# First expert's weights and two token tiles prepared in small pieces during the first MoE, no GpSimd sums from the border on, and second products taken as they are ready

## The chip, the core and the metric

One NeuronCore of one Trainium2 chip. The metric is the device time of one launch in microseconds; the kernel before has a median of 2106.39 us over three runs.

## What is computed

Three stages follow one another: causal attention with a decay bias, a dense MLP called here the first MoE, and an eight-expert MoE with balanced gates called the second MoE.

```python
def reference(q, k, v, s, w_in, w_out, w_gate, w1, w2):
    x = attention(q, k, v, s)               # 4 batches, 8 heads, 576 tokens, 64 wide
    x = x.transpose(0, 2, 1, 3).reshape(2304, 512)
    h = x @ w_in                            # 512 -> 2048
    x = (h * sigmoid(1.702 * h)) @ w_out    # 2048 -> 512
    logits = x @ w_gate                     # 8 experts
    P = np.exp(logits - logits.max())
    for _ in range(8):                      # rows and columns in turn
        P /= P.sum(1, keepdims=True) + 1e-9
        P /= P.sum(0, keepdims=True) + 1e-9
        P *= 2304 / 8
    out = 0
    for e in range(8):
        out += P[:, e:e+1] * (np.maximum(x @ w1[e], 0) @ w2[e])   # 512 -> 1024 -> 512
    return out
```

## The kernel before

The kernel is one program with five instruction streams. It does not issue its instructions where they are written: each call goes to a **planner** (class `Sequencer`, lines 51 to 246). The planner keeps a clock per engine and costs per operation (`cost`, line 120), holds DVE, ACT, POOL and SP operations back, and issues them in order of time; PE operations are issued at once. Of several operations that could go, the one of lower `rank` goes first, then the older one. `rank` 2 is for preparation that may wait. From `begin_second` on, `seq.fine` picks finer costs. All instructions therefore have one helper line in the profile, L261, and tiles tell them apart. On the chip each engine runs its own stream in the order the planner left, and semaphores do the waiting.

**Attention and first MoE** (to about 578 us of the span). PE takes attention units, transposes and MoE products as they come ready. The 2304 tokens of the first MoE are nine blocks of 256; the first seven run one by one. For a block and one of eight pairs of 256 hidden units, `mm1` makes `hp` (24 matmuls of 256 columns), ACT makes a tanh into `t`, DVE multiplies it with `hp`, ACT or DVE rounds it into `gh`, POOL subtracts for the rest `gl` (`any_less`), and `mm2` (line 984) adds 24 products into `acc`. The finished block goes through a tile `xo`, in the two-buffer ring `st` of `mpool`, to HBM (`x2_d`). The same ring, once the first MoE's weights are converted (about 190 us), is used to find the scales of expert 0's weights (`first_scales`, `more_scales`): eight loads of 512 KB, each with a DVE maximum.

**The border** (578 to 687 us). The last two blocks run together with 512 columns (`wide1`, `wide2`, lines 1019 to 1056): sixteen half pairs, each 12 matmuls into `hp` and 12 into `accw`. Beside them the planner places, at rank 2, what expert 0 needs: `prep_x(0)` and `prep_x(1)`, `prep_w2(0)`, `prep_w1(0, 0)`, `prep_w1(0, 1)` and then `weight_scales(1)`. A preparation loads four quarter matrices, forms the sums of a seven-product scheme (`seven`, `prep_w1`, `prep_x`), and turns each of the seven operands into a high and a low 16-bit half: ACT scales and rounds, DVE or POOL subtracts. For expert 0 the sums go to DVE or POOL, whichever has the shorter queue (`of_two`).

**Second MoE** (687 us on). For each of 8 experts and 3 token tiles of 768 there are four `unit1` (x times w1, seven products of 6 matmuls with 384 columns) and three `unit2` (h times w2, seven products of 12 matmuls with 256 columns). Two units are active at a time, on two sets of four PSUM banks A to D, and PE alternates between them by readiness. The seven results are combined by copying a bank and adding on to it: bank B starts as a copy of A, and C as a copy of B. Inside `unit2` (line 1504) the order of the products is written out: M1 (A), M7 (D), M2 (A), M6 (B), M5 (C), M4 (D), M3 (C). Only M1 and M7 may stop before the last quarter of `h`. The next expert's weights are prepared at rank 2 from `after1`: `weight_scales(e+1)` after tile 0, `prep_w2(e+1)` after tile 1, and `prep_w1(e+1, half)` after tile 2. Expert 0's start is different: `prep_x(2)` has rank 3 and comes first.

Of the kernel before, what the change touches and what calls it, by code (L numbers as in the profile page):

```python
# [9 lines left out]
F32 = mybir.dt.float32  # L10
# [21 lines left out]

POOL_BIAS = 3000
# [17 lines left out]
class Sequencer:  # L51
# [51 lines left out]
    def where(ap):  # L103
# [5 lines left out]
        hi = lo + sum((n - 1) * abs(st) for st, n in pairs[1:]) + 1  # L109
        return (p0, p0 + pairs[0][1]), (lo, hi)  # L110
# [9 lines left out]
    def cost(self, engine, what, out, ins):  # L120
        n = max(self.size(x) for x in [out] + ins[:2])
        psum = any(x.space == PSUM for x in ins)
        if self.fine:
            if engine == "PE":
                return self.size(out) * (4 if ins[0].dtype == F32 else 1) / 2.4 + (13 if ins[0].dtype == F32R else 5)
# [20 lines left out]
    def submit(self, engine, what, call, outs, ins):  # L146
# [8 lines left out]
        else:  # L155
            op.cost = self.cost(engine, what, outs[0], ins)
# [146 lines left out]
def kernel(  # L303
# [35 lines left out]
    early = const.tile([128, 41], F32, name="early")  # L339
# [10 lines left out]
    border = ExitStack()  # L350
# [633 lines left out]
    def mm2(i):  # L984
# [18 lines left out]
        if p == last and i == 1:  # L1003
# [3 lines left out]
            for m in range(2):  # L1007
                xo = mpool.tile([128, 2, TB1], F32, tag="st", name="xo", bufs=2)
# [27 lines left out]
    def wide2():  # L1036
# [8 lines left out]
        for m in range(KC):  # L1045
# [3 lines left out]
            if last:  # L1049
                xo = mpool.tile([128, 2, TB1], F32, tag="st", name="xo", bufs=2)  # L1050
# [155 lines left out]
    def first_scale(key, cols):  # L1206
# [9 lines left out]
        nc.vector.tensor_scalar(out=w[:, 1:2], in0=w[:, 0:1], scalar1=FLOOR, scalar2=None, op0=ALU.max)  # L1216
        b = w.bitcast(I32)
        nc.vector.tensor_scalar(
# [10 lines left out]

    def first_scales():  # L1230

        for i in range(8):
            st = mpool.tile([128, 1024], F32, tag="st", name="wm", bufs=2)
            if i < 4:
                v, s_ = "p (c f) -> p c f", w1[0, :, i * 256:(i + 1) * 256].rearrange("(c p) f -> p c f", p=128)
                st_ = st.rearrange(v, c=4)
            else:
                r = (i - 4) * 256
                st_ = st.rearrange("p (c d) -> p c d", c=2)
                s_ = w2[0, r:r + 256, :].rearrange("(c p) d -> p c d", p=128)  # L1240
            nc.sync.dma_start(out=st_, in_=s_)
            nc.vector.tensor_reduce(
                out=early[:, i:i + 1], in_=st, axis=AX.X, op=ALU.max, apply_absolute_value=True
            )
            yield st
            if i % 4 == 3:
                yield first_scale(("w1" if i < 4 else "w2", 0), early[:, i - 3:i + 1])
        q_of[0] = early[:, 40:41]
# [804 lines left out]
```

## Time and profile before

| | |
|---|---|
| runs | 2106.39, 2097.49, 2107.42 us (median 2106.39) |
| profiled execution | 2094.25 us, span 2092.5 us |
| PE busy | 1970.6 us (94%), 15782 matmuls recorded |
| DVE, ACT, POOL busy | 1407.9 us (67%), 1250.8 us (60%), 457.5 us (22%) |
| DMA | 317 MB, 152 GB/s on average |
| chain that ended last | PE 50%, issue 24%, DVE 11%, DMA 7%, POOL 4%, ACT 3% |

PE is the busiest engine; its matmuls are pipelined and their ends modelled, so a busy PE may still run below its best pace. A per-stage reading needs the stretches: before 190 us, to 578, to 687, to 950 and the rest. The engine names are PE (TensorE), DVE (VectorE), ACT (ScalarE), POOL (GpSimd) and SP (the queue that issues DMAs).

### The profile page before, as it was taken

The numbers are of one execution on the slowest core, as the hardware profiler recorded it, in microseconds if no ns is written. First come the engines' busy times: TensorE is split into PE (matmuls) and PEld (weight loads), VectorE is DVE, ScalarE is ACT, GpSimd is POOL, SyncE is SP. The second block draws the span as 40 slices with busy tenths as digits, with TensorE's granted clock in tenths as the row PEclk, the third lists the DMA queues.
The fourth block names the chain that finished last, engine by engine and source line by source line (L and its number), as shares of the span: only waits on it lengthen the run. The fifth ranks groups of instructions, "written<-read, shape, count | busy, mean of one in ns | idle before, by whom it ended". The sixth has DMA issues, their size and how long they took to land.

```text
span 2092.5 us, 41023 instructions
## 1 busy us (share of the span) xinstructions
PE 1970.6 (94%) x15782; PEld 1565.2 (75%) x15782; DVE 1407.9 (67%) x2927; ACT 1250.8 (60%) x2540; POOL 457.5 (22%) x473
## 2 busy tenths in 40 slices
PE   4888999999998999989999999999999999999998
PEld 3787999999986667756777777777767677777776
DVE  8987664754367656867875775675786677577555
ACT  5876554654445656565765656666676665566544
POOL 7775343453266121000001000000000000000000
PEclk9999999999999999999999999999999999999999
DMA  7554422331067635555666667648657566765331
GB/s 223 165 165 146 124 64 73 112 93 57 17 173 247 155 136 177 193 181 153 202 212 123 192 204 157 172 125 219 167 146 219 125 165 178 149 194 155 128 124 51
DMA packets 206232, 317.11 MB, mean 152 GB/s; under 512 B 20436, under 2 KB 134932, under 8 KB 206036
## 3 DMA queue, kind: packets, MB, share of 16 engines
q1 hardware_dynamic: 193076, 290.89, 43.8%
q0 software_dynamic: 12960, 23.60, 8.9%
q8 instruction: 124, 2.03, 0.4%
q14 instruction: 72, 0.59, 0.1%
HBM read 229.20 MB, written 80.68 MB: 148 GB/s over the span
## 4 chain that ended last, share of the span: by engine, by line
PE 50%; issue 24%; DVE 11%; DMA 7%; POOL 4%; ACT 3%; SPq 1%; POOLq 0%; ACTq 0%; DVEq 0%
PE C L261 9%; PE D L261 8%; PE A L261 7%; PE hp L261 7%; PE acc L261 6%; PE B L261 4%; DVE h L261 2%; PE sp L261 2%; POOL acc_d L261 2%; PE tp L261 2%; PE op L261 2%; DVE t L261 2%; DMA w_d<-wo 1%; DMA wm<-in_moe_w_dram 1%; DMA xc_d<-xo 1%
## 5 line engine op out<-in xcount | busy, mean ns | idle before, releaser
L261 PEld LDWEIGHTS <-h 128*128 128x128 f16 x6048 | 591.2, 98 | 134.7 <-issue 33.3
L261 PEld LDWEIGHTS <-w1o 128*128 128x128 f16 x4036 | 395.5, 98 | 270.8 <-issue 12.1
L261 POOL DMA_DIRECT2D acc_d<-y x90 | 77.9, 884 | 1050.9 <-DVE y L261 961.8
L261 PE MATMUL D<-xt,w1o 128*128 128x384 f16 x1152 | 218.9, 328 | 10.2 <-ACT w1o L261 8.2
L261 PE MATMUL A<-w2o,h 128*128 128x256 f16 x1728 | 216.2, 272 | 10.4 <-ACT B L261 10.4
L261 PE MATMUL C<-w2o,h 128*128 128x256 f16 x1728 | 210.1, 274 | 15.5 <-ACT C L261 12.2
L261 PE MATMUL D<-w2o,h 128*128 128x256 f16 x1728 | 220.7, 273 | 0.5 <-DVE h L261 0.5
L261 PE MATMUL C<-xt,w1o 128*128 128x384 f16 x1152 | 218.5, 326 | 1.9 <-DVE hst L261 1.2
L261 PE MATMUL A<-xt,w1o 128*128 128x384 f16 x1152 | 216.0, 326 | 0.3 <-DVE sc L261 0.3
L261 DVE SCALAR_TENSOR_TENSOR h<-hst,h 128x768 f16<-128x768 f32 (+1 forms) x192 | 144.3, 760 | 45.0 <-ACT h L261 42.9
L261 PE MATMUL hp<-xh,wih 128*128 128x256 f32 (+1 forms) x512 | 155.5, 304 | 3.9 <-DVE t L261 3.9
L261 PE MATMUL hp<-xl,wih 128*128 128x256 f32 (+1 forms) x512 | 153.0, 299 | 0.0
L261 PE MATMUL hp<-xh,wil 128*128 128x256 f32 (+1 forms) x512 | 152.8, 298 | 0.0
L261 ACT ACTIVATE h<-hst 128x768 f16<-128x768 f32 (+1 forms) x192 | 128.8, 678 | 6.7 <-DVE hst L261 6.7
L261 POOL TENSOR_TENSOR gl<-t,gh 128x512 fp32r<-128x512 f32 x72 | 96.9, 1346 | 159.8 <-ACT gh L261 109.5
L261 PE MATMUL B<-w2o,h 128*128 128x256 f16 x864 | 107.8, 275 | 15.6 <-DVE h L261 9.6
L261 ACT ACTIVATE sm<-sm,stats 64x576 f32<-64x576 f32 (+4 forms) x160 | 93.3, 602 | 43.9 <-DVE stats L261 42.9
L261 ACT ACTIVATE hst<-A 128x384 f32<-128x384 f32 x96 | 47.0, 489 | 121.2 <-PE A L261 120.4
L261 PE MATMUL acc<-gh,woh 128*128 128x256 f32 x384 | 111.0, 289 | 0.0
L261 PE MATMUL B<-xt,w1o 128*128 128x384 f16 x576 | 110.3, 328 | 0.0
L261 ACT ACTIVATE t<-hp 128x512 f32<-128x512 f32 x72 | 42.8, 594 | 112.5 <-PE hp L261 111.3
L261 ACT COPY B<-A 128x384 f32<-128x384 f32 (+1 forms) x168 | 70.5, 422 | 64.7 <-PE A L261 64.3
(243 smaller groups left out, 4254.4 us busy)
## 6 DMA issues: line engine op xcount, KB each, us to landing
xt<-xc_d SPq DMA_DIRECT2D x168, 384.0 KB
wr<-in_moe_w_dram SPq DMA_DIRECT2D x128, 256.0 KB
w_d<-wo SPq DMA_DIRECT2D x112, 256.0 KB
wm<-in_moe_w_dram SPq DMA_DIRECT2D x112, 256.0 KB
w2o<-w_d SPq DMA_DIRECT2D x56, 512.0 KB
acc_d<-y POOLq DMA_DIRECT2D x90, 256.0 KB, 5.6
kq<-in_qk_dram SPq DMA_DIRECT2D x32, 448.0 KB
kq<-in_qk_dram SPq DMA_DIRECT2D x32, 256.0 KB
```

Source lines behind the costliest of these rows:

```text
L261: self.seq.submit(self.name, what, lambda: method(*args, **named), outs, ins)
```

## The change

1. **Early pieces.** `first_scales` now also prepares expert 0 in the first MoE: w2 in four pieces and w1 in four (operands of 256 columns), then token tiles 0 and 1 in four pieces each (192 columns). A piece takes both buffers of the ring `st`; one loads, the other holds seven results that go to HBM. In pieces all sums and low halves are on DVE. The eight maxima for the scales become ACT squares.
2. **Border.** `prep_x(0)`, `prep_x(1)`, `prep_w2(0)` and `prep_w1(0, ..)` are gone from it; w1 of expert 0 is loaded ready from HBM in 14 transfers. `xo` moves from ring `st` to ring `t`.
3. **No POOL sums** from the border on: with `seq.fine`, `any_less` (and with it `gl`) is on DVE, and so are all sums.
4. **Expert 1 sooner.** `prep_w2(1)` is queued before expert 0 begins, with `prep_x(2)` ahead of it at rank 1.
5. **Products as ready.** `unit2` asks after each product which of those left is ready, in the order M1, M7, M2, M4, M6, M5, M3; every product may stop before the last quarter of `h`.
6. **Planner.** A range is counted in bytes, an operation with two outputs costs 190 more, and a fine PE matmul 2.7 instead of 5 above its columns. Sums reuse their inputs' buffers.

```diff
     def any_less(out, a, b, bias=POOL_BIAS):
-        engine = nc.vector if seq.load("DVE") + bias <= seq.load("POOL") else nc.gpsimd
+        engine = nc.vector if seq.fine or seq.load("DVE") + bias <= seq.load("POOL") else nc.gpsimd
...
     def of_two(out, in0, in1, op):
-        engine = nc.vector if seq.load("DVE") <= seq.load("POOL") else nc.gpsimd
-        engine.tensor_tensor(out=out, in0=in0, in1=in1, op=op)
+        nc.vector.tensor_tensor(out=out, in0=in0, in1=in1, op=op)
...
-                xo = mpool.tile([128, 2, TB1], F32, tag="st", name="xo", bufs=2)
+                xo = mpool.tile([128, 2, TB1], F32, tag="t", name="xo", bufs=2)
...
     def first_scales():
+        yield from early_scales(0)
+        for j in range(NJ):
+            yield early_w2(0, j)
+        for half in range(2):
+            for c in range(2):
+                yield early_w1(half, c)
+        yield from early_x(0)
+        yield from early_x(1)
...
+    def early_w2(e, j):
+        a, b = staged("wa"), staged("wb")
+        for fh in range(2):
+            r = fh * (F2 // 2) + j * 128
+            nc.sync.dma_start(out=a[:, fh * 512:fh * 512 + 512], in_=w2[e, r:r + 128, :])
...
+        def part(i, src):
+            o = out_slot(b, 256, 256, count_[0]).rearrange("p (h d) -> p h d", h=2)
+            count_[0] += 1
+            in_two(o[:, 0], o[:, 1], src, sc)
+            nc.sync.dma_start(out=w2_d[e % 2][i][:, :, j], in_=o)
+        seven([a[:, q * 256:q * 256 + 256] for q in range(4)], part, b[:, 0:256])
+        return b
...
     def begin_second():
-        prep_x(0)
...
-        prep_w2(0)
-        mem["raw"], mem["wo"] = (mem["ep"], 7), (mem["ep"], 2)
-        prep_x(1)
...
     def begin_weights():
         load_x2(0)
-        prep_w1(0, 0)
-        prep_w1(0, 1)
-        seq.rank = 3
-        weight_scales(1)
+        for half in range(2):
+            w1s[0, half] = pool.tile([128, 7, 2, 2, 256], F16, tag="w1o", name="w1o", bufs=2)
+            for i in (0, 6, 5, 3, 4, 1, 2):
+                nc.sync.dma_start(out=w1s[0, half][:, i], in_=w1_d[half][i])
+        second_expert()
...
     load_w2(0)
-    seq.rank = 3
+    seq.rank = 1
     prep_x(NTP - 1)
+    seq.rank = 2
+    prep_w2(1)
...
-        if tp == 1 and e + 1 < E:
+        if tp == 1 and 0 < e < E - 1:
             later(2, prep_w2, e + 1)
...
+        while todo:
+            yield lambda: min(x[0] for x in choices())
+            every = list(choices())
+            soon = max(min(x[0] for x in every), seq.free["PE"])
+            t, name, part = next(x for x in every if x[0] <= soon)
...
+            prod(bank[role], k, n, first=not before_, part=part)
+            if part[-1] == NJ - 1:
+                todo.remove(name)
+                after(name, bank[role])
+            else:
+                half_done.add(name)
```

How the streams move at three places follows; a row is one instruction with its tiles and size, in the order of its engine.

DVE at the border, early in the wide stage. `t` and `hp` belong to the first MoE, `wo`, `wr` and `wt` to expert 0's w2, `xo`, `xr` and `xt` to token tile 0. Before:

```order
L261 SCALAR_TENSOR_TENSOR t<-t,hp 128x512
L261 CAST gh<-t 128x512
L261 SCALAR_TENSOR_TENSOR wo<-wr,early,wo 128x512
L261 SCALAR_TENSOR_TENSOR wo<-wt_8791,early,wo 128x512
L261 TENSOR_TENSOR xo_8762<-xr,xo_8762 128x384
L261 SCALAR_TENSOR_TENSOR t<-t,hp 128x512
L261 CAST gh<-t 128x512
L261 TENSOR_TENSOR xo_8769<-xr,xo_8769 128x384
L261 SCALAR_TENSOR_TENSOR wo<-wr,early,wo 128x512 x2
L261 TENSOR_TENSOR xt_8768<-xt_8767,xr 128x384
L261 TENSOR_TENSOR xr<-xr 128x384
```

The same place now, where `xa` and `xb` are the two buffers of a piece of token tile 1:

```order
L263 SCALAR_TENSOR_TENSOR t<-t,hp 128x512
L263 TENSOR_TENSOR gl<-t,gh 128x512
L263 TENSOR_TENSOR xb<-xa,xb 128x192 x2
L263 SCALAR_TENSOR_TENSOR t<-t,hp 128x512
L263 TENSOR_TENSOR gl<-t,gh 128x512
L263 SCALAR_TENSOR_TENSOR t<-t,hp 128x512
L263 TENSOR_TENSOR xa<-xa 128x192 x2
L263 TENSOR_TENSOR gl<-t,gh 128x512
L263 TENSOR_TENSOR xb<-xa,xb 128x192 x2
L263 TENSOR_TENSOR xa<-xa 128x192
L263 TENSOR_TENSOR xb<-xa,xb 128x192 x3
L263 TENSOR_TENSOR xa<-xa 128x192
```

The rows of expert 0's weights are gone, `gl` has come over from POOL, and two of tile 1's four pieces are still here; later in the stage only `t`, `gh` and `gl` are left.

DVE at the start of expert 1. `hst`, `h`, `sa` and `sb` belong to a `unit1`; `w1o`, `wr` and `ws` are expert 1's second half of w1, which PE's third `unit1` of the expert reads. Before:

```order
L261 SCALAR_TENSOR_TENSOR w1o_11641<-wr_11645,sc5_9294,w1o_11641 128x512
L261 TENSOR_TENSOR h_12213<-sb_12215,h_12213 128x768
L261 TENSOR_TENSOR ws_11647<-wr_11642,ws_11646 128x512
L261 TENSOR_TENSOR wr_11644<-wr_11642,wr_11644 128x512
L261 TENSOR_TENSOR wr_11643<-wr_11643,ws_11647 128x512
L261 SCALAR_TENSOR_TENSOR w1o_11641<-ws_11646,sc5_9294,w1o_11641 128x512
L261 SCALAR_TENSOR_TENSOR w1o_11641<-ws_11647,sc5_9294,w1o_11641 128x512
L261 SCALAR_TENSOR_TENSOR w1o_11641<-wr_11644,sc5_9294,w1o_11641 128x512
L261 SCALAR_TENSOR_TENSOR w1o_11641<-wr_11643,sc5_9294,w1o_11641 128x512
L261 SCALAR_TENSOR_TENSOR hst_12283<-D0_12260,u2_12267 128x384
```

Now, at the first two `unit1` of expert 1 (`hst` of D0, then of D1):

```order
L263 SCALAR_TENSOR_TENSOR hst_12296<-D0_12265,u2_12272 128x384
L263 SCALAR_TENSOR_TENSOR w1o_11859<-wr_11862,sc5_9582,w1o_11859 128x512
L263 SCALAR_TENSOR_TENSOR hst_12296<-C0_12284,m7_12273 128x384
L263 SCALAR_TENSOR_TENSOR w1o_11859<-wr_11860,sc5_9582,w1o_11859 128x512
L263 SCALAR_TENSOR_TENSOR w1o_11859<-wr_11863,sc5_9582,w1o_11859 128x512
L263 SCALAR_TENSOR_TENSOR w1o_11859<-ws_11864,sc5_9582,w1o_11859 128x512
L263 TENSOR_TENSOR wr_11861<-wr_11861,wr_11860 128x512
L263 SCALAR_TENSOR_TENSOR h_12354<-hst_12296,h_12354 128x384
L263 TENSOR_TENSOR sa_12355<-hst_12296 128x384
L263 SCALAR_TENSOR_TENSOR h_12354<-hst_12296,h_12354 128x768
L263 SCALAR_TENSOR_TENSOR hst_12375<-D1_12333,u2_12340 128x384
```

Before, the third unit's join (`hst_12283`, the fifteenth join in all) stood behind five `w1o` rows; now one `w1o` row is left behind the fourteenth join.

PE inside the first pair of `unit2` of a later expert's tile, around the first matmul of M6 (bank B of set 1). The number behind `h` is one of the four quarters of the hidden width; 21214 before and 21388 now are the last. Before:

```order
L261 LDWEIGHTS h_21214
L261 MATMUL D0_21288<-w2o_20268,h_21214 128x256
L261 LDWEIGHTS h_21214
L261 MATMUL D0_21288<-w2o_20268,h_21214 128x256
L261 LDWEIGHTS h_20981
L261 MATMUL B1_21284<-w2o_20268,h_20981 128x256
```

Now:

```order
L263 LDWEIGHTS h_21388
L263 MATMUL D1_21425<-w2o_20443,h_21388 128x256
L263 LDWEIGHTS h_21388
L263 MATMUL D1_21425<-w2o_20443,h_21388 128x256
L263 LDWEIGHTS h_21153
L263 MATMUL B1_21469<-w2o_20443,h_21153 128x256
```

Before, M6 came right behind the last quarter of M7 (D0); now the 12 matmuls of M2 (bank A of set 0) and the 12 of M4 (D1) stand between that quarter and M6.

## Rows read from the trace of the kernel before

**Rows 1.** Busy time of each engine by stretch (x: instructions), granted clock, DMA share.

```profile
100.00:190.00 90.00, 76.93 (x733) 69.85 (x731) 80.34 (x195) 68.23 (x139) 61.35 (x58) 0.98 0.52 159
190.00:578.00 388.00, 386.01 (x3778) 368.63 (x3779) 212.43 (x674) 195.07 (x368) 155.98 (x177) 0.99 0.27 80
578.00:687.00 109.00, 97.13 (x417) 76.99 (x416) 75.40 (x93) 56.60 (x116) 65.86 (x47) 0.97 0.67 209
687.00:850.00 163.00, 153.41 (x1247) 109.57 (x1247) 108.81 (x221) 95.13 (x197) 21.66 (x19) 0.98 0.49 151
850.00:950.00 100.00, 83.19 (x623) 61.80 (x621) 68.83 (x147) 58.63 (x126) 0.00 (x0) 0.93 0.60 198
950.00:1950.00 1000.00, 970.34 (x7344) 716.76 (x7343) 694.33 (x1241) 639.53 (x1325) 77.91 (x90) 1.00 0.64 170
```

**Rows 2.** Timeline of PE in the border (start, us), then the gate's matmuls.

```profile
581.68 0.40 PE L261 MATMUL hp<-xh,wih 128*128 128x512 f32 x1
...
611.17 0.39 PE L261 MATMUL accw<-gh,woh 128*128 128x512 f32 x1
...
613.89 0.39 PE L261 MATMUL hp<-xh,wih 128*128 128x512 f32 x1
...
L261 PE MATMUL gp<-wgs,xt x180: 169/169/221, 687.0 to 821.7; 128*128 128x16 f16 x180
```

**Rows 3.** What PE waited for, 578 to 687 us (total us, times, longest).

```profile
PE accw L261 <- POOL gl L261: 8.5, 8, 2.1
PE accw L261 <- DVE gh L261: 3.3, 2, 1.8
```

**Rows 4.** What PE waited for, 687 to 950 us.

```profile
PE D L261 <- ACT w1o L261: 8.2, 1, 8.2
PE A L261 <- ACT B L261: 4.2, 4, 3.1
PE B L261 <- ACT h L261: 4.1, 3, 1.8
...
PE B L261 <- DVE h L261: 2.5, 3, 1.3
...
PE D L261 <- DVE w1o L261: 1.0, 1, 1.0
```

**Rows 5.** Busy time by stretch of 10 us, where PE stood longest.

```profile
900.00:910.00 10.00, 4.53 (x14) 1.92 (x15) 6.89 (x11) 4.19 (x7) 0.00 (x0) 0.50 0.49 151
```

**Rows 6.** What PE waited for, 950 us to the end.

```profile
PE C L261 <- ACT C L261: 11.4, 12, 2.3
PE B L261 <- DVE h L261: 7.1, 11, 0.8
...
PE B L261 <- ACT h L261: 1.9, 5, 0.4
```

**Rows 7.** Groups of instructions, shapes apart: busy us, mean ns of one, idle before.

```profile
L261 DVE SCALAR_TENSOR_TENSOR w1o<-wr,sc,w1o 128x512 f16<-128x512 f32 x70 | 50.2, 745 | 1.1 <-ACT w1o L261 1.1
L261 DVE SCALAR_TENSOR_TENSOR y<-C,pq,y 128x256 f32<-128x256 f32 x63 | 30.4, 482 | 113.8 <-PE C L261 92.6 <-ACT m L261 12.4 <-ACT y L261 7.5
L261 DVE SCALAR_TENSOR_TENSOR w1o<-wr,early,w1o 128x512 f16<-128x512 f32 x10 | 13.4, 1368 | 4.3 <-ACT w1o L261 4.3
L261 DVE TENSOR_REDUCE early<-wm 128x1 f32<-128x1024 f32 x8 | 9.7, 1218 | 4.8 <-DMA wm<-in_moe_w_dram 4.8
L261 DVE TENSOR_TENSOR ws<-wr 128x512 f32<-128x512 f32 x14 | 9.6, 684 | 0.5 <-DMA wr<-in_moe_w_dram 0.5
L261 ACT ACTIVATE wm<-wm 128x512 f32<-128x512 f32 x112 | 69.2, 621 | 32.2 <-DMA wm<-in_moe_w_dram 32.1
L261 ACT ACTIVATE y<-C,pq 128x256 f32<-128x256 f32 x62 | 29.0, 468 | 117.8 <-PE C L261 110.8 <-DVE y L261 6.9
```

**Rows 8.** POOL's costliest group, in the same view.

```profile
L261 POOL TENSOR_TENSOR gl<-t,gh 128x512 fp32r<-128x512 f32 x72 | 96.9, 1346 | 159.8 <-ACT gh L261 109.5 <-DVE gh L261 39.1 <-issue 4.1
```

**Rows 9.** DMA issues on SP: duration of one issue, ns min/median/max, first and last start.

```profile
L261 SPq DMA_DIRECT2D xc_d<-xo x42: 319/322/571, 593.1 to 802.3; - x42
```

More of the change, by code (lines that the diff above doesn't have):

```diff
@@ new lines, in one_scale, with early_x, out_slot @@
+    def one_scale(key, cols, squares=False):
+        if "small" in mem:
+            scale_of(key, cols, squares)
+        else:
+            yield first_scale(key, cols, squares)
+    def early_x(tp):
+        yield 3 * tp + 3
+        yield from one_scale(("x", tp), xmx[:, 6 * tp:6 * tp + 6])
+        for c in range(2):
+            for q in range(2):
+                yield early_x_part(tp, c, q)
+    def out_slot(b, at, n, i):
+        return b[:, at + i % (5 if n == 192 else 3) * n:][:, 0:n].bitcast(F16)
@@ new lines, in early_w1, with part @@
+    def early_w1(half, c):
+        a, b = staged("wa"), staged("wb")
+        piece = {}
+        for fh in range(2):
+            for kh in range(2):
+                x = a[:, (2 * fh + kh) * 256:(2 * fh + kh) * 256 + 256]
+                r, f0 = (2 * kh + c) * 128, fh * (F2 // 2) + half * 256
+                nc.sync.dma_start(out=x, in_=w1[0, r:r + 128, f0:f0 + 256])
+                piece[fh, kh] = x
+        sc = sc_of["w1", 0]
+        count_ = [0]
+        def part(i, src):
+            o = out_slot(b, 256, 256, count_[0]).rearrange("p (h d) -> p h d", h=2)
+            count_[0] += 1
+            in_two(o[:, 0], o[:, 1], src, sc)
+            nc.sync.dma_start(out=w1_d[half][i][:, :, c], in_=o)
+        four(piece, part, b[:, 0:256])
+        return b
@@ L1568, in unit2 @@
         before = {}
-        most, last = range(NJ - 1), range(NJ - 1, NJ)
-        yield ready(0, 0, free("A"), part=most)
-        past[s] = False
-        a = bank_tile("A", s)[:, 0:256]
-        prod(a, 0, 0, part=most)
-        yield ready(3, 6, free("D"), part=most)
-        d = bank_tile("D", s)[:, 0:256]
-        prod(d, 3, 6, part=most)
-        yield ready(0, 0, part=last)
-        prod(a, 0, 0, part=last)
-        b = bank_tile("B", s)[:, 0:256]
-        nc.scalar.copy(out=b, in_=a)
@@ L1581, in unit2 @@
-        y0, y1 = (mem["st"].tile([128, DM], F32, tag="y", name="y", bufs=4) for _ in range(2))
-        whole_d = ready(3, 6, part=last)
-        done_d = whole_d() <= seq.free["PE"]
-        if done_d:
-            prod(d, 3, 6, part=last)
-            put(y1[:, 256:512], d, t1)
-        yield ready(2, 1, settled(a))
-        prod(a, 2, 1, first=False)
-        put(y0[:, 0:256], a, t0)
-        past[s] = True
-        if not done_d:
-            yield whole_d
-            prod(d, 3, 6, part=last)
-            put(y1[:, 256:512], d, t1)
@@ L1608, in unit2, with of, add @@
-        leave(t1, y1)
-        yield ready(6, 2, settled(c))
-        prod(c, 6, 2, first=False)
-        put(y0[:, 256:512], c, t0)
-        leave(t0, y0)
+        bank, y, begun = {}, {}, set()
+        def of(t, half):
+            if t not in y:
+                y[t] = mem["st"].tile([128, DM], F32, tag="y", name="y", bufs=4)
+            return y[t][:, half * 256:half * 256 + 256]
+        def add(o, t, half):
+            if (t, half) in begun:
+                more(of(t, half), o, t)
+            else:
+                begun.add((t, half))
+                put(of(t, half), o, t)
@@ new lines, in unit2, with at @@
+        steps = {
+            "M1": ("A", 0, 0, ()), "M7": ("D", 3, 6, ()), "M2": ("A", 2, 1, ("M1",)), "M4": ("D", 1, 3, ("M7",)),
+            "M6": ("B", 5, 5, ("M1",)), "M5": ("C", 4, 4, ("M6",)), "M3": ("C", 6, 2, ("M5",)),
+        }
+        todo = list(steps)
+        half_done = set()
+        def at(name, part):
+            role, k, n, before_ = steps[name]
+            if any(x in todo for x in before_):
+                return never
+            if name in half_done or before_:
+                t = ok(bank[role])
+            else:
+                t = bank_free(role, s)
+            return max(t, ready(k, n, part))
```

241 lines of the change are left out of this document (143 added, 98 removed).

## The prediction

> **What bounds the kernel now.** I read the busy time by stretch first, then what PE waited for in each, then the groups with shapes apart for prices. The stretches say where PE has something to lose [rows 1]. From 190 to 578 us, attention and first MoE, it is busy 386.0 of 388.0 us: it sets the pace, and DVE (212.4 us, 55%) and ACT (195.1 us, 50%) hide beside it. The border, 578 to 687 us, leaves it idle 11.9 of 109 us; 687 to 950 us, expert 0 and the start of expert 1, 9.6 and 16.8 us; the thousand behind that 29.7 us, 3%. So the time lies in the border and expert 0, and there is little anywhere else.
>
> Border: the first wide matmul starts at 581.68 us, the gate's first at 687.0 us, 105.3 us later. At full pace 12 of them take 613.89 - 611.17 = 2.72 us [rows 2], so the 16 x 24 take 87.0 us. 18.3 us are lost: 11.8 in waits, of them 8.5 for `gl` on POOL [rows 3], the rest in a granted clock of 0.97 and in starts. Expert 0 to 950 us: 9.2 us for expert 1's `w1o`, 4.2 for the copy of A into B, 6.6 for parts of `h` [rows 4]; in the 10 us of the long wait the granted clock is 0.50, that is the lower of the two levels, 1.2 GHz [rows 5], after an idle stretch; PE is busy 4.53 us there, so about 2.3 us of it are the clock's. Later: 9.0 us of waits of bank B for `h`, 11.4 us for the copy of B into C [rows 6].
>
> **The change, part by part.**
>
> *Border.* What leaves: expert 0's w2 and w1 and tile 0, with their halves and sums, and POOL. What comes: `gl` at 0.68 us on DVE (an SBUF sum of 512 columns, [rows 7]) for 1.35 us on POOL [rows 8], two pieces of tile 1, the squares for expert 1, and 14 loads of w1. DVE then has per half pair a multiplication, sometimes a copy, and `gl`, under 2.2 us of the 5.44 us that 24 matmuls take, and 24 piece operations, under 0.5 us each. PE needs `gl` a whole wide product later than `hp` was done, so I see nothing left to wait for. I take 15 of the 18.3 us; bounds 8 (the 8.5 us of `gl` waits) and 18.
>
> *POOL beside DVE.* The same `w1o` instruction takes 1368 ns for expert 0, beside POOL, and 745 ns for the later experts, when POOL is quiet [rows 7]. That supports the border term. It speaks against the early pieces, which put two-input SBUF work beside POOL. The Trainium skill (SBUF — State Buffer, Who interferes with whom) says that a VectorE instruction with two SBUF inputs and a GpSimd instruction that reads SBUF exclude each other for a whole instruction; the two rows agree.
>
> *Early pieces in the first MoE.* Eight pieces of w2 and w1 and six of tiles 0 and 1 fall before 578 us (the other two are seen at the border). On DVE: 7 low halves for each of the 14 pieces, 98, and 4 sums each, 56: 154 instructions of 256 or 192 columns. None is in the trace alone; the nearest row is 482 ns for 256 columns, which I use for all, 74 us, less 8 x 1.218 us of maxima, 64 us. On ACT: 98 roundings at 468 ns, 46 us, eight squares of 1024 columns at about twice the 621 ns of 512, 10 us, and six scalings of 768 columns at 0.9 us, 5 us: 61 us [rows 7]. DVE goes from 212 to 277 us (71% of 388), ACT from 195 to 256 us (66%). Beside POOL a two-input operation cost 1368 - 745 = 0.62 us more where POOL was busy 60% (65.9 of 109); at the 40% it has here that is 0.4 us, which would bring 63 us more and DVE to 88%. SP gets 48 loads and 98 stores more, at 0.32 us or a little over each [rows 9]: some 50 us of a queue that only issues; but a store that waits for a late DVE half holds the loads of `kq`, `va` and `two` behind it, and so attention. What does PE lose? Nothing if the cover of the 190 to 578 stretch holds; 54 us if it becomes like 100 to 190 us, where DVE is busy 89%, ACT 76% and PE idle 13.1 of 90 us, 14% [rows 1]. I take 10 us, nearer to nothing: an operation in the way is about 0.5 us long, the planner gives it low rank, and attention gives PE other work. Both ends stay for the range. `xo` in ring `t` makes the tanh two items on wait for a store, at most 7 times; it is within that.
>
> *Expert 0.* `prep_w2(1)` runs from the start of expert 0 and not after its tile 1, so DVE and ACT come to expert 1's `w1o` with w2 behind them, and five rows that stood ahead of the third unit have shrunk to one. The 9.2 us and the clock's 2.3 us should go. What hides the new place: with the squares of expert 1 still at the border and no more POOL sums, DVE has room in 687 to 850 us (108.8 of 163, [rows 1]). Of the 6.6 us for `h` I take 4, of the 4.2 us for B 1.5 (the one of 3.1 us came behind the same backlog). Together 17; bounds 4 and 24 us.
>
> *Products as ready.* M6 moves 24 matmuls away from the last quarter of `h`, as the order shows; that covers waits of 0.8 us at the longest. I take 8 of the 9.0 us from 950 us on. C's 11.4 us stay: C still starts 12 matmuls or fewer after B has ended. M3 has lost M4 as a spacer and can wait for the add that reads C. Bounds: 5 us lost, 20 gained (all the 20.4 us of [rows 6]).
>
> *Planner's numbers, reused buffers, factors:* orders change, work does not; nothing.
>
> **Sum.** -15 (border) -17 (expert 0) -8 (later) +10 (first MoE) = -30 us. The profiled execution's 2094.25 us becomes 2064. It is the fastest of the four times shown; their three runs have a median of 2106.39, which would become 2076. I predict 2070 us, between the two.
>
> **Rivals.**
> 1. *DVE and POOL share more than they spare.* By the 0.4 us above for each of 154 operations DVE is at 88% in the first MoE, and PE waits for its halves, its tanh products and the attention maxima as in 100 to 190 us: +54 - 40 = +14 us, 2108 from the profiled time, 2120 from the median. It decides once PE's idle share there passes 10%, 40 us. For it: the pair 1368/745. Against it: the operations are half as wide, and POOL is idle 60% of the stage. This is also what the skill's rule would give if every meeting cost a whole instruction.
> 2. *The border waits for transfers instead of halves.* 14 loads of w1 (256 KB each) and 7 of tile 0 (384 KB), 6.3 MB, go out in the second half of the wide stage. At the 209 GB/s of the border [rows 1] they take 30 us; half of the stage lasts 43.5 us. If they start late behind the pieces' stores, the first unit waits up to 30 us, border and half of expert 0 are given back: 2088 to 2095. Against it: nothing else that is large goes at that time, and the squares' loads come behind them.
> 3. *Waits only move.* `w1o` of expert 1 stays late, since the buffer of its second half comes free at the same point as before, and C waits more: border 12, expert 0 5, later 0, first MoE 10 lost: -7 us, 2087 to 2099.
>
> That the order is as described is seen in the streams; what it gives is open.
>
> **How the numbers follow.** A measurement of this kernel tells 0.5%, about 10.5 us, from no change. My forecast, 18 to 55 us gained, has 0.62; rival 3 has 0.16 and rival 2 0.09, half of these within 10.5 us of no change; rival 1 has 0.13, nearly all of it slower. So faster 0.73, same 0.14, slower 0.13. The likeliest case alone spans 2040 to 2086. The range goes on to 2106, into rivals 2 and 3; its low end is 2038 (first MoE 0, border 18, expert 0 24, later 14 from the profiled time). About 0.06 is left below and 0.13 above.
>
> **What would show it.** Right: PE's span from the first wide matmul to the gate near 90 us, no wait for `gl`; no wait of D for `w1o` above 1 us near 870 us, no 0.50 clock there; B's waits for `h` under 2 us after expert 0; DVE 65 to 80% and PE idle 5 to 15 us between the last conversion and the border, `wb` and `xb` halves above 0.5 us where POOL is at work. Wrong: PE idle over 40 us before the border (rival 1); a wait of the first unit for `xt` or `w1o` transfers (rival 2); `w1o` again in the list, or C's waits up by as much as B's went down (rival 3).

## The result and the profile after

The changed kernel takes 2044.72 us in the median of four runs (2038.97 to 2050.68), the kernel before 2106.90 us (four runs, 2097.49 to 2113.19). The ratio is 0.972, 95% interval 0.968 to 0.975: 62 us less where the sum forecast 30. The time lies inside the range of 2038 to 2106 us, near the low end of the likeliest case and 25 us under the 2070 us forecast.

The two profiled executions differ by less. That of before, 2094.25 us, is below all four of its timed runs; that of the changed kernel, 2050.68 us, is the highest of its four. Between their spans lie 43.5 us, and with a second profiled execution of the changed kernel (`after_again` below, span 2037.7 us) 54.8 us. What the longer runs of the kernel before do with their 3 to 19 us more no profile here shows.

The stretches below are cut at the same four events in each kernel: the first wide matmul, the gate's first matmul, and the first copy of a bank A into `hst` in expert 1 and in expert 2. Columns: stretch, length, then busy us and instructions of PE, weight loads, DVE, ACT and POOL, granted clock, DMA share, GB/s. The kernel before:

```profile
190.00:581.68 391.68, 389.69 (x3807) 372.11 (x3808) 212.85 (x675) 195.96 (x370) 155.98 (x177) 0.99 0.27 79
581.68:687.00 105.32, 93.45 (x387) 73.51 (x386) 74.98 (x92) 55.71 (x115) 65.86 (x47) 0.97 0.69 216
687.00:886.50 199.50, 186.21 (x1504) 135.44 (x1504) 138.50 (x290) 115.42 (x237) 21.66 (x19) 0.97 0.52 163
886.50:1069.80 183.30, 168.06 (x1260) 123.32 (x1259) 134.72 (x246) 113.47 (x233) 0.00 (x0) 0.97 0.58 181
1069.80:2092.50 1022.70, 989.34 (x7524) 734.52 (x7522) 678.12 (x1203) 628.79 (x1311) 77.91 (x90) 1.00 0.60 160
```

The changed kernel, same columns:

```profile
190.00:593.68 403.68, 395.19 (x3863) 376.31 (x3862) 286.24 (x832) 256.35 (x520) 167.15 (x184) 0.99 0.44 127
593.68:681.20 87.52, 87.52 (x388) 71.78 (x387) 34.17 (x73) 34.52 (x81) 0.00 (x0) 1.00 0.52 156
681.20:865.40 184.20, 180.36 (x1507) 134.03 (x1507) 137.46 (x302) 118.47 (x237) 0.00 (x0) 1.00 0.52 173
865.40:1031.30 165.90, 164.37 (x1257) 122.60 (x1255) 130.24 (x233) 110.15 (x229) 0.00 (x0) 1.00 0.62 193
1031.30:2049.00 1017.70, 990.24 (x7524) 737.30 (x7522) 685.97 (x1240) 624.45 (x1287) 77.78 (x90) 1.00 0.60 161
```

Stretch by stretch: the first MoE ends 12.0 us later, the border is 17.8 us shorter, expert 0 15.3, expert 1 17.4, the rest 5.0. The border has PE busy for all of its 87.52 us, within 0.6 us of the 87.0 us of full pace worked out ahead. In experts 0 and 1 the gain has two halves, and the second is easily overlooked: PE's idle time falls from 13.3 + 15.2 to 3.8 + 1.5 us, 23.2 less, and for the same number of matmuls (1504 and 1507, 1260 and 1257) PE is also busy 5.9 + 3.7 us less, because the granted clock is 1.00 in place of 0.97 (3% of the 382.8 us of both experts is some 11 us of clock).

In the border no wait of PE is left; [rows 3] has no counterpart. What PE waited for in expert 0 (two longest rows), in expert 1 (all), and from 950 us on (all), in the changed kernel:

```profile
PE B L263 <- ACT xo L263: 0.8, 1, 0.8
PE A L263 <- DVE h L263: 0.7, 1, 0.7
```

```profile
PE C L263 <- ACT C L263: 1.1, 2, 0.6
PE A L263 <- ACT B L263: 0.3, 1, 0.3
```

```profile
PE A L263 <- ACT B L263: 14.3, 16, 4.0
PE C L263 <- ACT C L263: 7.8, 13, 1.0
PE C L263 <- DVE y L263: 0.6, 1, 0.6
```

Against [rows 4], the waits for `w1o` and those of B for `h` are gone. Against [rows 6], the waits of B for `h` are gone too, and A's for its copy into B have more than doubled. Before, from 950 us on:

```profile
PE A L261 <- ACT B L261: 6.2, 18, 0.8
```

The early pieces in the groups of DVE and ACT, 0 to 600 us (busy us, mean ns of one, idle before):

```profile
L263 DVE SCALAR_TENSOR_TENSOR wb<-wa,early,wb 128x256 f16<-128x256 f32 x48 | 28.3, 599 | 15.1 <-ACT wb L263 15.0
L263 DVE TENSOR_TENSOR xb<-xa,xb 128x192 f16<-128x192 f32 x42 | 23.7, 590 | 3.6 <-ACT xb L263 3.5
L263 DVE TENSOR_TENSOR wa<-wa 128x256 f32<-128x256 f32 x16 | 10.8, 677 | 0.2
L263 DVE TENSOR_TENSOR xa<-xa 128x192 f32<-128x192 f32 x24 | 9.6, 402 | 8.0 <-ACT xa L263 7.7
...
L263 ACT ACTIVATE wb<-wa,early 128x256 f16<-128x256 f32 x48 | 23.3, 502 | 17.7 <-DVE wa L263 7.8 <-DMA wa<-in_moe_w_dram 7.0 <-DMA w_d<-wb 2.4
```

With the four smaller groups the 154 operations keep DVE busy for 88.4 us; one takes 585 ns in the mean. The last two of token tile 1's pieces fall into the border, where POOL does nothing, and there the same instruction is far shorter (590 ns above):

```profile
L263 DVE TENSOR_TENSOR xb<-xa,xb 128x192 f16<-128x192 f32 x14 | 4.4, 352 | 3.7 <-ACT xb L263 3.7
```

Taken one by one in the trace, 84 of the 154 have no POOL instruction beside them and take 404 ns in the mean, none over 489; the other 70 overlap one and take 801 ns, up to 1705. Shape by shape, 27 us of the time of the 154 go to that.

### The profile page after: what moved, and what is told of

Its sections match the earlier page's. It is cut to its first block, busy times and chain, and to the rows that moved or that the text cites. A ratio compares the mean times of both kernels' runs of the same rounds, so it can differ in the third digit from the quotient of the medians.

```text
span 2049.0 us, 41389 instructions
## 1 busy us (share of the span) xinstructions
PE 1964.9 (96%) x15782; PEld 1571.4 (77%) x15782; DVE 1437.2 (70%) x3072; ACT 1276.5 (62%) x2615; POOL 371.5 (18%) x410
## 4 chain that ended last, share of the span: by engine, by line
PE 67%; issue 11%; DVE 9%; DMA 8%; ACT 4%; POOL 1%; SPq 0%; DVEq 0%; ACTq 0%; POOLq 0%
PE C L263 13%; PE D L263 13%; PE A L263 12%; PE hp L263 8%; PE B L263 7%; PE acc L263 4%; DVE t L263 2%; PE sp L263 2%; DMA wm<-in_moe_w_dram 2%; PE op L263 2%; PE accw L263 2%; PE tp L263 2%; DVE h L263 2%; DMA w_d<-wo 1%; DMA acc_d<-y 1%
## 5 line engine op out<-in xcount | busy, mean ns | idle before, releaser
L263 PE MATMUL D<-w2o,h 128*128 128x256 f16 x1728 | 214.6, 273 | 0.5 <-ACT y L263 0.5
L263 PE MATMUL C<-w2o,h 128*128 128x256 f16 x1728 | 205.0, 272 | 10.2 <-ACT C L263 8.9
L263 ACT COPY C<-B 128x384 f32<-128x384 f32 (+1 forms) x168 | 71.5, 425 | 82.3 <-PE B L263 65.3
L263 PE MATMUL acc<-gl,woh 128*128 128x256 f32 x384 | 108.5, 283 | 0.0
L263 PE MATMUL acc<-gh,wol 128*128 128x256 f32 x384 | 108.4, 282 | 0.0
```

The lines of the kernel that those rows point to most:

```text
L263: self.seq.submit(self.name, what, lambda: method(*args, **named), outs, ins)
```

## The experiments

The kernels ran in three groups, each beside runs of the kernel before on the same chip, whose medians were 2105.37, 2111.84 and 2096.52 us; ratios are therefore compared, not times. This table gathers all of them (expert 0 runs from the gate's first matmul; us, from the profiled executions; the ratio is that of the timed runs).

| kernel | first wide matmul | border | expert 0 | expert 1 | rest | ratio, 95% interval |
|---|---|---|---|---|---|---|
| before | 581.7 | 105.3 | 199.5 | 183.3 | 1022.7 | 1 |
| after_again | 590.6 | 87.5 | 184.3 | 166.3 | 1009.0 | 0.9719 (0.9695 to 0.9742) |
| unit2_fixed | 591.2 | 87.5 | 188.3 | 176.0 | 1029.1 | 0.9848 (0.9825 to 0.9871) |
| w2_late | 592.1 | 87.5 | 185.5 | 167.9 | 1016.2 | 0.9731 (0.9708 to 0.9753) |
| gl_pool | 590.7 | 88.7 | 183.3 | 174.4 | 1013.0 | 0.9747 (0.9723 to 0.9772) |
| ready_only | 583.4 | 107.4 | 200.9 | 183.1 | 1017.1 | 0.9896 (0.9865 to 0.9927) |
| no_pool_only | 582.3 | 103.0 | 213.9 | 181.4 | 1035.5 | 1.0033 (1.0009 to 1.0057) |
| no_pieces | 586.9 | 102.1 | 215.3 | 188.3 | 1021.0 | 1.0041 (1.0017 to 1.0064) |
| old_costs | 594.7 | 93.4 | 181.7 | 167.8 | 1038.1 | 0.9822 (0.9785 to 0.9858) |
| pieces_only | 595.4 | 94.5 | 188.9 | 171.4 | 1036.8 | 0.9944 (0.9923 to 0.9965) |
| no_190 | 597.3 | 90.8 | 183.5 | 169.9 | 1021.9 | 0.9846 (0.9817 to 0.9875) |
| wm_late | 589.2 | 87.4 | 185.6 | 174.3 | 1004.2 | 0.9747 (0.9720 to 0.9775) |
| halves_twice | 600.9 | 88.9 | 188.7 | 169.7 | 1012.5 | 0.9840 (0.9811 to 0.9869) |

The two profiles of the changed kernel itself differ by 8.7 us in the rest and 3.1 at the first wide matmul, so smaller differences in these columns are not read. The profile of after_again is the shortest of its six executions, 9 us under their median, so what another kernel's rest loses against it is an upper bound; against the first profile it is 8.7 us less.

**after_again**: no edit.

> The changed kernel once more, unaltered, as the measure for the others. In its first profile the granted clock was 0.87 from 0 to 100 us and 0.83 from 100 to 150 us, where the kernel before had 1.00, 0.97 and 1.00; the first wide matmul came at 593.68 us, 12.0 us later than before. If the low clock of the first 150 us belongs to the change (its other order of the attention there), it is there again and the first wide matmul is at 592 to 596 us. If it belongs to that one execution, the clock is 0.95 to 1.0 and the first wide matmul comes at 586 to 590 us, so that the early pieces cost some 6 us and not 12. On both readings the border lasts 87 to 88 us and the ratio to the kernel before is 0.968 to 0.975.

The clock was 0.86, 0.90 and 0.86 in the three stretches of 50 us, so the low clock is in both profiles of the changed kernel; how much of it is the change's is taken up in the last section. The first wide matmul came at 590.56 us, between the two expectations, and the border was 87.5 us again.

**unit2_fixed**: the products' order.

```diff
-        while todo:
-            yield lambda: min(x[0] for x in choices())
...
+        yield ready(0, 0, free("A"), part=most)
+        prod(a, 0, 0, part=most)
+        yield ready(3, 6, free("D"), part=most)
+        prod(d, 3, 6, part=most)
...
+        yield ready(5, 5, settled(b))
+        prod(b, 5, 5, first=False)
...
```

> The changed kernel with the second units' products in the order written out before, only M1 and M7 stopping ahead of the last quarter. My theory (readiness hides the waits of bank B for h): these waits, 0 us from expert 2 on in the changed kernel, are 6 to 10 us again, experts 2 to 7 take 5 to 8 us more, experts 0 and 1 another 2 to 4 us, 8 to 12 us in all (0.4 to 0.6%). Rival (the waits only move between banks, since the waits of A for the copy in B rose from 5.8 to 14.3 us): those fall back to about 6 us, and the time stays within 3 us. Second rival (the gain of the start of expert 1 is the order's): 15 to 25 us more, most of it in experts 0 and 1.

The ratio rose by 1.3%, 27 us: the second rival's size, but not its place. Experts 0 and 1 took 4.0 and 9.7 us more, the rest 20.1 (11.4 against the first profile). What PE waited for in the rest:

```profile
PE B L263 <- DVE h L263: 10.8, 14, 1.1
PE C L263 <- ACT C L263: 9.1, 5, 2.6
PE B L263 <- ACT h L263: 5.7, 9, 1.0
PE A L263 <- ACT B L263: 4.8, 5, 3.0
```

B's waits for `h` are 16.5 us from expert 2 on, where [rows 6] has 9.0 from 950 us on, so the written order does worse inside the changed kernel than it did in the kernel before. In expert 1 one wait of C for `y` took 5.2 us. There was no wait for `w1o`.

**w2_late**: expert 1's w2 where it was.

```diff
-    seq.rank = 2
-    prep_w2(1)
     seq.rank = 0
...
-        if tp == 1 and 0 < e < E - 1:
+        if tp == 1 and e + 1 < E:
             later(2, prep_w2, e + 1)
```

> The changed kernel with expert 1's w2 prepared after tile 1 of expert 0, as for the later experts, and nothing else undone. My theory (the early w2 is what brought w1o in time): PE waits 6 to 10 us for w1o at the start of expert 1 with a clock of about 0.5 behind it, expert 1 takes 9 to 14 us more, the whole 9 to 14 us more (0.45 to 0.7%). Rival (with the pieces and the squares done before, DVE and ACT have room for w2 and w1 of expert 1 in a row at any time): no wait for w1o over 1 us, the whole within 3 us.

The rival held. The ratio is 0.973 against 0.972, expert 1 took 1.6 us more, and PE did not wait for `w1o` at all. The early w2 is not what brought `w1o` in time.

**gl_pool**: POOL allowed again.

```diff
-        engine = nc.vector if seq.fine or seq.load("DVE") + bias <= seq.load("POOL") else nc.gpsimd
+        engine = nc.vector if seq.load("DVE") + bias <= seq.load("POOL") else nc.gpsimd
```

> The changed kernel with the planner again free to put gl and the other low halves of any_less on POOL from the border on. My theory (in the border it was the preparations beside POOL, not POOL by itself, that made gl late): border 87.5 to 91 us, waits for gl under 3 us, the low halves of token tile 2 on POOL cost nothing that shows; the whole 0 to 4 us more. Rival (a gl of 1.35 us on POOL is late by itself): waits of 6 to 9 us for gl again, border 94 to 98 us, the whole 7 to 10 us more.

My theory held in the border: with all 16 `gl` back on POOL it took 88.7 us, and of the 8.5 us of waits for `gl` this is left:

```profile
PE accw L263 <- POOL gl L263: 1.1, 2, 0.5
```

Expert 1 took 8.1 us more, most of it in waits of about 1 to 2.5 us of A, C and D for ACT and DVE; the whole is 0.3% longer, with an interval that overlaps the changed kernel's.

**ready_only**: the kernel before with the changed `unit2` and nothing else (the diff of `unit2` above the prediction).

> The kernel before with the second units' products taken as ready and nothing else changed. The changed kernel lost 27 us when it went back to the written order, 14 of them in experts 0 and 1 and most of the rest in experts 3 to 6. If readiness is worth as much on its own, the kernel before gains 20 to 28 us (ratio 0.987 to 0.990), with the border at 105 us as before and the waits of B for h gone. Rival (readiness needs the planner's new PE cost, since the old one of 5 above the columns lets it see products ready later or earlier than they are): 4 to 12 us gained (0.994 to 0.998). Second rival (the wait for w1o at the start of expert 1 has nothing to do with the products): it stays at 8 us or more, and experts 0 and 1 together gain under 5 us.

The gain was 1.0%, 20 to 22 us, as expected, but the second rival's condition is met too: the wait for `w1o` stays, and experts 0 and 1 do not shrink.

```profile
PE D L261 <- ACT w1o L261: 7.0, 1, 7.0
...
PE D L261 <- DVE w1o L261: 1.0, 1, 1.0
```

So readiness pays by itself, and the wait for `w1o` does not depend on it. Against the one profile of the kernel before, the shortest execution of its group, this gain does not show (2092.5 and 2091.9 us); it stands on the timed runs.

**no_pool_only**: the kernel before with part 3 alone.

```diff
-        engine = nc.vector if seq.load("DVE") + bias <= seq.load("POOL") else nc.gpsimd
+        engine = nc.vector if seq.fine or seq.load("DVE") + bias <= seq.load("POOL") else nc.gpsimd
...
-        engine = nc.vector if seq.load("DVE") <= seq.load("POOL") else nc.gpsimd
-        engine.tensor_tensor(out=out, in0=in0, in1=in1, op=op)
+        nc.vector.tensor_tensor(out=out, in0=in0, in1=in1, op=op)
```

> The kernel before with gl, the low halves of any_less and all sums on DVE from the border on, and nothing else changed; the preparations of expert 0 stay in the border. My theory of the border (POOL and its sharing with DVE made gl late): waits for gl under 3 us, the border 93 to 98 us, 7 to 12 us less. Rival (the border's vector work as a whole is too much: DVE takes on 60 us of POOL's work at about half its duration, 30 us more on 75): the waits for gl and gh stay or grow, border 103 to 112 us, and w1o of expert 0 or 1 comes 5 to 20 us later.

The rival held: 0.3% slower. The border is 103.0 us, expert 0 14.4 us longer, and PE still waits for `gl`, now on DVE, and at the start of expert 0 bank B waits until ACT has copied the first MoE's last result out of it, into `xo`:

```profile
PE accw L261 <- DVE gl L261: 11.0, 2, 10.6
```

```profile
PE B L261 <- ACT xo L261: 8.3, 1, 8.3
```

**no_pieces**: the kernel before with parts 3, 5 and 6, so without the early pieces, the early w2 and the reused buffers.

> The kernel before with the sums on DVE, the products as ready and the planner's new numbers, so the changed kernel without the early pieces, the early w2 of expert 1 and the reused buffers. If the pieces carry the border and the room in experts 0 and 1, then this kernel has its first wide matmul 6 to 10 us sooner than the changed one (582 to 586 us), a border of 95 to 105 us, and 2065 to 2080 us in all. Rival (the pieces only shift work, and the sums on DVE with the products' order are what helps): border under 92 us and the whole at 2040 to 2052 us, as the changed kernel or below.

The first theory held in direction and was far too small: 0.4% slower than the kernel before, 3.2% slower than the changed one. The border waits 11.2 us for `gl` on DVE; in experts 0 and 1 (two fences):

```profile
PE A L263 <- DMA xt<-xc_d: 11.5, 2, 8.7
PE B L263 <- ACT xo L263: 8.7, 1, 8.7
```

```profile
PE D L263 <- ACT w1o L263: 10.0, 1, 10.0
```

The wait for `w1o` is there at its longest. The granted clock is 0.95 in the border and 0.94 in expert 0. With the pieces (and the early w2 and the reused buffers, which come back together with them) all of this goes: the border falls by 14.6 us, expert 0 by 31.0, expert 1 by 22.0 (against after_again).

**old_costs**: two of the planner's numbers.

```diff
-                return self.size(out) * (4 if ins[0].dtype == F32 else 1) / 2.4 + (13 if ins[0].dtype == F32R else 2.7)
+                return self.size(out) * (4 if ins[0].dtype == F32 else 1) / 2.4 + (13 if ins[0].dtype == F32R else 5)
...
-            op.cost = self.cost(engine, what, outs[0], ins) + (190 if len(outs) > 1 else 0)
+            op.cost = self.cost(engine, what, outs[0], ins)
```

> The changed kernel with two of the planner's numbers as before: 5 instead of 2.7 above the columns of a fine matmul, and no 190 for a second output. My forecast put the numbers at nothing: the whole within 4 us, the clock of the first 150 us 0.86 to 0.90 again. Rival 1 (the 190, which sits on the softmax's ACT operations, has changed the order of the attention and with it the clock there): clock 0.97 to 1.0 in the first 150 us, first wide matmul at 582 to 587 us. Rival 2 (the PE cost of 2.7 is what lets readiness choose well): experts 2 to 7 take 5 to 12 us more.

The forecast of nothing fell: 1.0% more. The border lost 5.9 us, the rest 29 (20 against the first profile); the clock of the first 150 us is 1.00, 0.97, 1.00, as before the change, and yet the first wide matmul comes no sooner, at 594.7 us.

**pieces_only**: the changed kernel with the edits of unit2_fixed, w2_late, gl_pool and old_costs together. The sums stay on DVE and the buffers reused, so it holds a little more than the pieces.

> The changed kernel with only the early pieces left (and the reused buffers): products in the written order, expert 1's w2 after tile 1, POOL allowed for gl and low halves, the planner's numbers as before. Without the pieces the rest of the change gave nothing (ratio 1.004). If the pieces carry experts 0 and 1 by taking the preparation off DVE and ACT there, then the border is 88 to 95 us, the opening and expert 0 together take 182 to 190 us (199.5 before, 215 with the sums on DVE and no pieces), no wait for w1o at the start of expert 1, experts 2 to 7 as before, and the ratio is 0.978 to 0.988. Rival (pieces and products help only together, since it is the last quarter of h that the preparation delays): ratio 0.990 or above, the waits of B for h in experts 0 and 1 stay at 6 us or more, and the gain is the border's alone, less the first MoE.

The pieces give 0.6%, 11 to 12 us, the rival's size; but the stretches are those of the theory. Opening and expert 0 take 188.9 us, expert 1 171.4, no wait for `w1o` is left, the border is 94.5. It is the other columns that take it back: the first wide matmul is 13.7 us later than before and the rest 14.1 us longer.

**no_190**: the second output's cost alone taken out.

```diff
-            op.cost = self.cost(engine, what, outs[0], ins) + (190 if len(outs) > 1 else 0)
+            op.cost = self.cost(engine, what, outs[0], ins)
```

> The changed kernel without the 190 for a second output, the PE cost of 2.7 kept. With both numbers old the time rose by 1.0% of the kernel before, the granted clock of 0 to 150 us was 1.0, 0.97, 1.0 instead of 0.86, 0.90, 0.86, the border 93.4 us and experts 3 to 6 some 7 us longer each. If the 190 makes the low clock (it sits on the softmax and the squares) and the 2.7 the later gain: clock 0.97 to 1.0 in 0 to 150 us, experts 2 to 7 in 1009 to 1018 us, the border between 87.5 and 93 us. The first MoE: if the low clock costs time, the first wide matmul is at 584 to 588 us and the whole 3 to 6 us under the changed kernel; if the shorter planned softmax is what makes DVE and ACT late, it is at 592 to 596 us as with both numbers old, and the whole 2 to 10 us over it.

The ratio rises by 1.3%, and with both numbers old it was 1.0%, with intervals that overlap: the 2.7 shows no gain of its own, the 190 does. Its row was in the profile of the kernel before, unread, and in the changed one it is the same. The kernel before, then the changed one, then the second outputs of the attention's reductions on DVE in the changed one (the larger of two groups):

```profile
L261 ACT ACTIVATION_READ_ACCUMULATOR wm<-wm 128x1 f32 x112 | 21.3, 190 | 0.0
L263 ACT ACTIVATION_READ_ACCUMULATOR wm<-wm 128x1 f32 x120 | 22.8, 190 | 0.0
L263 DVE DVE_READ_ACCUMULATOR2_ANT stats<- 128x1 f32 x128 | 10.1, 79 | 0.0
```

Each square leaves its column sum through a second ACT instruction of 190 ns, 16 of them per expert, 3 us. The planner's 190 also falls on the second outputs of the attention's reductions, which are DVE's and take 79 ns, so there the plan has gone from too little to too much. Why the number is worth 1.3% is argued and not shown: a planner that does not know of the squares' second instruction lets ACT run behind its plan, and the copies of the banks stand in that queue. The waits of A for its copy are the longest of all in the rest of no_190, but only 3 to 7 us above the changed kernel's 14.3 and 10.4 us:

```profile
PE A L263 <- ACT B L263: 17.0, 20, 5.1
```

The clock of the first 150 us is back, without a gain in the first MoE (597.3 us). no_190 first, the changed kernel behind it:

```profile
0.00:50.00 50.00, 23.50 (x130) 17.70 (x130) 41.27 (x107) 29.39 (x64) 36.30 (x48) 1.00 0.70 218
50.00:100.00 50.00, 43.67 (x441) 38.95 (x441) 46.31 (x122) 43.23 (x78) 38.03 (x37) 0.96 0.54 174
100.00:150.00 50.00, 45.95 (x447) 42.37 (x445) 43.72 (x120) 36.49 (x78) 32.41 (x33) 0.94 0.50 159
```

```profile
0.00:50.00 50.00, 24.51 (x136) 18.16 (x137) 38.83 (x104) 30.19 (x66) 34.52 (x50) 0.87 0.68 212
50.00:100.00 50.00, 44.18 (x427) 38.78 (x425) 42.29 (x109) 40.96 (x75) 33.54 (x33) 0.86 0.51 159
100.00:150.00 50.00, 43.99 (x403) 40.32 (x404) 45.36 (x115) 36.06 (x76) 31.68 (x33) 0.83 0.48 146
```

**wm_late**: an attempt to go below the changed kernel. In after_again ACT stands for a load of the squares while the copy of A into B waits behind it, and PE waits for the copy (timeline; us from the start, duration, idle time before in brackets):

```profile
1578.20 0.63 ACT L263 ACTIVATE wm<-wm 128x512 f32<-128x512 f32 x1 [4.41 <-DMA wm<-in_moe_w_dram]
...
1578.83 0.74 ACT L263 COPY B<-A 128x256 f32<-128x256 f32 x2
...
1579.24 1.47 PE L263 MATMUL A<-w2o,h 128*128 128x256 f16 x12 [2.54 <-ACT B L263]
```

```diff
             st = raw([128, 1, DM], "wm")
+            seq.late = 3000
             nc.sync.dma_start(out=st, in_=w2[e, i * 128:(i + 1) * 128, :].rearrange("p (o d) -> p o d", o=1))
+            seq.late = 0.0
             squares(mx[:, 1, i:i + 1], st)
...
```

> An attempt to beat the changed kernel. ACT waits for the loads of the next expert's squares (wm) 20.2 us in ten places from expert 2 on, up to 4.4 us, and what stands behind it on ACT is the copy of bank A into B: at 1579.24 us PE waits 2.54 us for it. This kernel lets the planner count these loads (and nothing else) 3 us later, so that the squares are placed behind work that is ready. If that is the cause of most of the remaining waits: A's waits for the copy in B 2 to 5 us instead of 10 to 14, C's 3 to 5, the whole 6 to 12 us less. Rival (the squares then stand before other copies, or the loads come late by as much again since their buffers come free later): the waits move, the whole within 4 us.

The cause was right and the gain did not come. In the rest A's waits for the copy fell from 10.4 to 0.3 us and C's from 5.6 to 2.6, those of C for `y` rose to 4.8, and the rest is the shortest of all, 1004.2 us. But expert 1 took 8.0 us more:

```profile
PE C L263 <- DVE hst L263: 4.6, 1, 4.6
```

The ratio, 0.9747, is not distinguishable from the changed kernel's 0.9719. No kernel here is shown to be better than the changed one.

**halves_twice**: the low halves of the eight weight pieces formed twice.

```diff
             in_two(o[:, 0], o[:, 1], src, sc)
+            nc.vector.scalar_tensor_tensor(
+                out=o[:, 1], in0=src, scalar=sc, in1=o[:, 0], op0=ALU.mult, op1=ALU.subtract
+            )
```

> The changed kernel with the low halves of the eight weight pieces formed twice, 56 more operations of 256 columns on DVE in the first MoE at 599 ns, 34 us of DVE time. DVE had 284 of 400.6 us there (71%) and would have some 318 (79%). Where PE's cover holds (my theory of the first MoE), the first wide matmul comes 0 to 6 us later and nothing else moves. If DVE is near its limit there (the rival that DVE and POOL share more than they spare), it comes 15 to 35 us later and PE's idle time between 190 us and the border rises from 7 to over 20 us.

In between. DVE was busy 22 to 24 us more there, the first wide matmul came 7 to 10 us later, and PE's idle time doubled, from 6.8 and 8.5 us to 14.4:

```profile
190.00:600.90 410.90, 396.54 (x3871) 378.04 (x3870) 308.74 (x870) 257.36 (x523) 168.20 (x183) 0.99 0.43 123
```

The pieces then also end too late: at the start of expert 0 B waited 6.2 us for `xo`. Together it cost 1.2%. The cover in the first MoE is not free but sloped: by this one step, some 0.3 to 0.4 us per us of DVE.

## Why the prediction was right, and where its sums failed

The direction, the range and the picture of where the time lies were right: border and expert 0 gained, the first MoE paid. The sum of -30 us was -43.5 between the two profiles and -54.8 with the second. That the time fell into the range was in part luck: the low end of 2038 us takes the best bound of every term, 56 us, from the profiled execution, and the medians lie 62 us apart. The start from 2094.25 us, the shortest execution of its group, made up for a sum that was too small.

- *Border, -15 forecast, -17.8 measured:* nothing was left to wait for, so it came at the far bound of 18. Of the two reasons named, preparation leaving and `gl` leaving POOL, the first is enough by itself. Without the pieces, `gl` on DVE made PE wait as much (11.0 us); with them, `gl` on POOL cost 1.1 us. What made `gl` late is the preparation beside it, on whichever engine.
- *Expert 0 and the start of expert 1, -17 forecast, -32.7 measured (opening, experts 0 and 1), beyond the far bound of 24.* The step that failed is the one that credited the early `prep_w2(1)`: w2_late shows no wait for `w1o` without it. The wait goes with the pieces: it is in ready_only, no_pool_only and no_pieces, and not in pieces_only (which keeps the reused buffers too). The size failed at two terms: I left some 8 us of the waits standing that went as well, and booked 2.3 us for the clock, around the long wait alone, where PE's busy time fell by 9.5 us over both experts.
- *Products as ready, -8 forecast.* Taken out of the changed kernel it costs 1.3%, 27 us; put into the kernel before it gives 1.0%, 21 us. The rows priced only B's waits for `h`; the term was mis-sized by more than half. A written order waits in other places too (C for `y`, 5.2 us at once in unit2_fixed); where the rest of the 21 to 27 us lies no run separates. That C's waits would stay was about right (7.8 after 11.4 us), that A's would grow to 14.3 (10.4 in the second profile) was not seen.
- *Planner's numbers, nothing forecast.* The step "orders change, work does not; nothing" fell clearly: the 190 is worth 1.3%. For the squares it is a true duration that the plan had left out; for the attention's reductions on DVE it is not (79 ns). What it does to the kernel before by itself was not run; in no_pieces it stands beside readiness and sums on DVE, and that kernel is 0.4% slower than before. Whether the reused buffers cost something, as the longer rest of pieces_only may hint, was not tried.
- *First MoE, +10 forecast, +12.0 and +8.9 measured.* Right in size, and composed otherwise: no_pieces, without pieces but with the new numbers, is 5.2 us later than before, and the pieces add 4 to 7; without the new numbers (pieces_only) they add 13.7, so the split depends on what stands beside them. The 154 operations took 585 ns in the mean, 0.10 us over the 482 booked, but that hides what sharing cost: 66 of them have 192 columns and not 256, without a POOL instruction beside them they take 404 ns in the mean, and POOL, busy 41% of the stretch, adds 0.17 us to each, 27 us in all, where rival 1 had 0.4 us and 63. At the slope of halves_twice, 27 us of DVE would be 8 to 11 us of PE, as much as the whole term; that is an estimate, and no run takes the sharing out. The Trainium skill (SBUF — State Buffer, Who interferes with whom) has a VectorE instruction with two SBUF inputs shut out for a whole GpSimd instruction when the two meet. The trace agrees: the 70 operations that overlapped a POOL instruction, whose mean there is 918 ns, took 801 ns in place of some 400.

The rivals: the first (DVE and POOL) did not come as a whole. Its mechanism did, at some 40% of its size, while PE's idle share there is 2.1%, not 10. The second (transfers) did not come: there is no wait for `xt` or for a load of `w1o` at the start of expert 0, while the preparation in the border does have it, 11.5 us in no_pieces. The third (waits only move) is half seen: from 950 us on A's waits for the copy grew from 6.2 to 14.3 us as B's 9.0 for `h` went; but the time did not stay.

The parts do not add up. Singly, pieces give 0.6%, products 1.0%, no POOL sums -0.3%; all together 2.8%. My reading is that each part ends a wait behind which another stood; the runs show the difference, not its cause. The 190 without the other parts, and the reused buffers, were not tried.

## What to carry to other kernels

Preparation that moves into an underused stage was worth more here than the waits it removed in the busy stage, since the granted clock came back with them (0.97 to 1.00 in experts 0 and 1): price the stage by PE's busy time per matmul as well as by its idle time. In a kernel whose order is planned, a cost that the plan leaves out can show in the time (here a number of 190 ns, worth 1.3%), so compare the plan's costs with the profile's rows before moving work. Price an instruction on DVE by a row with POOL as busy as it will be (352 and 590 ns here for the same one). And undo one part at a time: the part that was credited with the gain here gave none.

## What was not expected of the hardware

The granted clock in the first 150 us was 1.00, 0.97 and 1.00 by stretches of 50 us without the 190 (old_costs) and 0.86 to 0.87, 0.86 to 0.90 and 0.83 to 0.86 in the two profiles of the changed kernel. From 100 to 150 us it follows the planned order: 0.83 to 0.87 in all eight profiles with the 190, which run the same instructions in the same order there, and 0.93 to 1.00 in the six without. From 0 to 50 us it does not: of those same eight, w2_late, wm_late, no_pieces and halves_twice have 1.00 and the other four 0.86 to 0.87. What decides that, no run shows. The low clock did not set the end of the stage: without the 190 the first wide matmul is 3.6 to 6.7 us later (no_190), not sooner. And an ACT square with a column sum is two instructions, 1062 and some 190 ns for 1024 columns.
